# Masked scores written back to their PSUM bank in a banded attention chain, with a new instruction order

## The chip, the cores and the metric

One core of one Trainium2 chip runs the kernel. The metric is device time in microseconds (us) of one execution; the kernel was timed in three runs.

## What is computed

Attention with 16 heads-times-batches of 768 positions and 64 channels, followed by two dense layers pairs on the 1536 tokens of 512 channels that come out of it.

```python
scores = scale * np.matmul(q, k.transpose(0, 1, 3, 2))
keep = is_sink | in_window            # 4 sink columns, a causal window of 128
scores = np.where(keep, scores, -1e9)
scores = scores - np.max(scores, axis=-1, keepdims=True)
a = np.exp(scores)
a = a / (np.sum(a, axis=-1, keepdims=True) + 1e-09)
x = np.matmul(a, v)                   # -> (1536, 512)
h = x @ w_in                          # 512 -> 2048
g = np.where(h >= 1, h, np.where(h <= -1, 0, (h + 1) ** 2 / 4))
y = g @ w_out                         # 2048 -> 512
gate = 1 / (1 + np.exp(-(y @ w_gate)))
out = (gate * (y @ w_val)) @ w_out2   # 512 -> 1536 -> 512
```

## The kernel before

**Tiling.** The window is so narrow that 112 queries see 16 sink columns and at most 240 others, so a tile of 112 queries (the last of a batch has 96) has at most 256 columns of keys. Two batches of 7 tiles give tiles 0 to 13. Each tile is worked in four *slots* (`p`), and a slot is a pair of heads (`e` is 0 or 1). The first tile of a batch has 128 columns instead of 256.

**One slot.** TensorE (PE) multiplies queries and keys of both heads into two PSUM banks (`scores`, L927); two slots share these two banks, each taking one half (`j`) of both. VectorE (DVE) adds the mask, multiplies by -0.125 and takes the row minimum in one custom instruction (`top`, L930, by the helper at L1186), which writes the scaled scores to the SBUF tile `pr`. ScalarE (ACT) takes exponentials with that minimum as bias and sums the rows (`exp`, L933), in place in `pr`; a second short instruction reads out the sum. PE transposes the result into a PSUM tile (`turn`, L941), ScalarE copies that to SBUF (`pts`, by the helper at L358), and PE multiplies with the values (L968), for four slots in one piece. So a full tile has 8 tops, 8 exponentials, 4 copies of `pts`.

**End of a tile.** VectorE inverts the row sums `sm` (L982, L983), some engine widens them to `ie` (a copy), PE transposes `ie` (L991), ScalarE copies the output out of PSUM to `on`, VectorE multiplies the two (L1003), and `on` is split into `xh` and the remainder `xl` (L365), the two halves that the dense layers multiply with. A copy may be placed on ScalarE (L358), VectorE (L360) or GpSimd (POOL, L362).

**The dense layers.** The rest of the kernel is nearly all PE work: each product is three matmuls (high by high, high by low, low by high). The first stage for the first 512 tokens (`block`, L551 to L553 and L596 to L598, in pieces of 6 and 9 matmuls) is interleaved with the attention; its first piece needs `xl` of tile 4. Weights come as raw words (`st`, 512 KB each) on SyncE's DMA queue, behind queries, keys and values, and each is rebuilt on ScalarE or GpSimd (L452, L454), then in four VectorE instructions (L457 to L466), then split in two.

**Order.** Every step is an `op` with an engine (or several to choose from), an assumed duration, a due time, and keys that it reads and writes. A list scheduler (`Plan.order`) walks through assumed time: when an engine is free it starts the ready step with the earliest due time, and when a step can go on several engines it takes the one that ends first, with `BIAS` added. The order in which it starts steps is the order in which instructions are written out, and each engine executes its own in that order. `FINISH`, `MOE_DUE`, `MOE_PACE`, `EARLY`, `LATE`, `SAME_MODE` shift due times. Buffers are rings; PSUM's 8 banks are shared by scores, transposes, outputs and the dense layers, and a bank is given out again when its last user in the plan has ended. The real waits are set by the framework below, from the memory that each instruction touches; for PSUM it counts a whole bank as one.

Of the kernel before, what the change touches and what calls it, by code (L numbers as in the profile page):

```python
# [14 lines left out]
AF = mybir.ActivationFunctionType  # L15
# [3 lines left out]
P = 128  # L19
# [33 lines left out]
START = {"ACT": 0.9, "DVE": 2.1, "PE": 1.0, "SP": 1.1}  # L53
READY = {"tops": 0.2, "next": 0.5, "values": 1.5}

BIAS = {"DVE": 0.38, "POOL": 0.06, "ACT": -0.07}

SLOT_DUE = 2.55

FINISH = {"top": 3.59, "exp": 11.24, "turn": 13.87, "pts": 4.86, "values": -2.54, "div": 5.08, "out": -6.02}  # L60
MOE_DUE = 65.7
MOE_PACE = 5.86
DRAIN = 8.5
EARLY = 15.01
LATE = 62.91

ENTER, LEAVE = {"rows": 0.18, "cols": 0.14}, 0.09
SCORES_OF = 2
VALUES_OF = 4
SAME_MODE = 4.27  # L70
WARM = 6
RAW = 3
POOL_FROM = 5
# [11 lines left out]
def a_us(n):  # L85
    return 0.093 + n / 1200


def d1_us(n):
    return 0.068 + n / 1920  # L90


def d2_us(n):
    return 0.068 + n / 960


def g1_us(n):
    return 0.16 + n / 1195
# [14 lines left out]
def cells(name, row, c0, c1):  # L113

    return [(name, row, c) for c in range(c0 // 16, -(-c1 // 16))]
# [26 lines left out]
class Plan:  # L142
# [11 lines left out]
    def op(self, eng, dur, due, fn, reads=(), writes=(), lat=0.0, after=(), port=False, mode=None, uses=()):  # L154
        o = Op()
        o.on = eng if isinstance(eng, dict) else {eng: dur}
        o.pick = isinstance(eng, dict)

        o.port = port or "POOL" in o.on
        o.due, o.fn, o.lat, o.mode = due, fn, lat, mode  # L160
        o.n, o.deps, o.next, o.new = len(self.ops), set(after), [], []
        o.start = o.end = None
        for k in reads:
            if k in self.writer:
                o.deps.add(self.writer[k])
            self.readers.setdefault(k, []).append(o)
        for k in writes:
            if k in self.writer:
                o.deps.add(self.writer[k])
            elif isinstance(k, Buf) and not k.users:  # L170
                o.new.append(k)
            o.deps.update(self.readers.get(k, ()))
            self.writer[k], self.readers[k] = o, []
        o.deps.discard(o)

        o.new += [k for k in uses if not k.users]
        o.bufs = {k for k in (*reads, *writes, *uses) if isinstance(k, Buf)}
        for k in o.bufs:
            k.users.append(o)
        self.ops.append(o)  # L180
        return o

    def order(self):
# [16 lines left out]
        def room(o, t):  # L200
            if any(b.users[0] is not o and b.users[0].start is None for b in o.bufs):
                return False
            for b in o.new:
                r = b.ring
                if b.at - r.taken >= sum(c.ring is r for c in o.new):
                    return False
                if b.at >= r.n and not over(r.asked[b.at - r.n], t):
                    return False
            return all(len(idle(b.ring, t)) >= len(o.new) for b in o.new if b.ring.banks)
# [9 lines left out]
        def begin(o, e):  # L219

            t = max(free[e], now)
            return max(t, held["POOL" if e == "DVE" else "DVE"]) if o.port and e in held else t

        def best(o, e):

            return all(begin(o, x) + o.on[x] + BIAS.get(x, 0.0) >= begin(o, e) + o.on[e] + BIAS.get(e, 0.0) for x in o.on if x != e)

        while done < len(self.ops):
# [13 lines left out]
            for e in engines:  # L242
                if free[e] > now:
                    continue
                can = [(o.due - (SAME_MODE if e == "PE" and o.mode == mode else 0.0), o.n, o) for t, o in ready[e] if t <= now and best(o, e) and room(o, now)]
                if not can:
# [56 lines left out]
class Body:  # L303
# [205 lines left out]
    def W(self, nm, i, due):  # L509

        while self.asked <= self.first[nm, i]:
            self.load(*self.loads[self.asked], due - (EARLY if self.asked < 2 * STAGES[0] else LATE))
            self.asked += 1
# [326 lines left out]
    def banded(self):  # L840


        nc, NP, op, pre = self.nc, self.NP, self.plan.op, self.pre
# [16 lines left out]
        ot_r = self.bank_ring(OT_BANKS, P, NP, TQ)  # L860
        moe_due = [MOE_DUE, MOE_PACE]
        D = P // 2
        ot = sm = sc = None

        def slot(k, due):
            nonlocal ot, sm, sc
            t, p = slots[k]
            b, i, q0, n = tiles[t]
            ks = 1 if i == 0 else 2
            at = 1 if t < RAW else i % 2  # L870
            mask = masks.of(i, at)
# [26 lines left out]
            j = p % 2  # L898
# [4 lines left out]
            banks, o, sums = sc, ot, sm  # L903
            pt, pts = Buf(pt_r), Buf(pts_r)
            pr, mx = (Buf(pr_r), Buf(mx_r)) if t else (Kept(pre["rows"](p)), Kept(pre["mx"][:, 2 * p:2 * p + 2]))
            in_ring = [pr, mx] if t else []
            at_pr = [] if t else cells("acc", 0, pre["pr"][p], pre["pr"][p] + 2 * P)
# [19 lines left out]
                    nc.tensor.matmul(out=out, lhsT=own()[es, :n], rhs=rhs, start=True, stop=True)  # L927

            def top(e):
                row_tops(nc, pr.ap[:n, e, :ks * P], banks[e].ap[:n, j, :ks * P], mask[:n, :ks * P], mx.ap[:n, e:e + 1])  # L930

            def exp(e):
                nc.scalar.activation(  # L933
                    out=pr.ap[:n, e, :ks * P], in_=pr.ap[:n, e, :ks * P], func=AF.Exp,
                    bias=mx.ap[:n, e:e + 1], scale=-1.0, accum_out=sums.ap[:n, 2 * p + e:2 * p + e + 1],
                )

# [5 lines left out]
            f, m = ks / 2, ks * P  # L943
            if t:
                yield 0.43 * f, scores, rq, [(x, j) for x in sc], sc
            for e in range(2):
                if t == 0:
                    op("PRE", 0.0, 0.0, lambda: None, [], [(pr, e), (mx, e)], lat=READY["tops"] + 0.22 * (2 * p + e))
                    continue
                tops.append(op("DVE", d2_us(m) + 0.01, due - FINISH["top"], lambda e=e: top(e), [(banks[e], j), ("mask", min(i, 2))], [(pr, e), (mx, e)], uses=[banks[e], *in_ring]))  # L950
            for e in range(2):
                op("ACT", a_us(m) + 0.185, due - FINISH["exp"], lambda e=e: exp(e), [(mx, e)], [(pr, e), (sums, 2 * p + e), *at_pr], uses=[*in_ring, sums])
            op("PE", 0.38 * f + 0.02, due - FINISH["turn"], turn, [(pr, 0), (pr, 1), *at_pr], [pt], uses=in_ring[:1])

            def take(e):
# [5 lines left out]

            op({"ACT": a_us(4 * f * n), "DVE": d2_us(4 * f * n)}, 0, due - FINISH["pts"], take, [pt], [pts])

# [11 lines left out]
            if p == NP - 1:  # L975
# [21 lines left out]
                m = NP * n  # L997
                op("DVE", 0.28, due - FINISH["div"], inverse, [(sm, h) for h in range(H)], [sm], port=True)
                pool = t >= POOL_FROM
                op(self.some(pool, ACT=a_us(NP * P), DVE=d1_us(NP * P), POOL=g1_us(NP * P)), 0, due - FINISH["div"], widen, [sm], [ie], port=True)  # L1000
                op("PE", 0.38, due - FINISH["div"], spread, [ie], [ib])
# [12 lines left out]
        tops = []  # L1014
        for k in range(0, len(slots), NP):
            if k == NP:
                op("DVE", 1.25, SLOT_DUE * (NP - 2), masks.make_second, [], [("mask", 1)])
            if k == 2 * NP:
                op("DVE", 0.6, SLOT_DUE * (2 * NP - 2), masks.make_others, [("mask", 1)], [("mask", 2)])
            tile = [slot(k + j, SLOT_DUE * (k + j)) for j in range(NP)]  # L1020
            for j in range(0, NP if k else 0, SCORES_OF):
                both(tile[j:j + SCORES_OF], SLOT_DUE * (k + j), "rows")
                if VALUES_OF == 2:
                    both(tile[j:j + 2], SLOT_DUE * (k + j + 1) - FINISH["values"], "cols")
            if VALUES_OF == NP:
                both(tile, SLOT_DUE * (k + NP - 1) - FINISH["values"], "cols")
            for x in tile:
                next(x)
# [156 lines left out]
def row_tops(nc, out, x, mask, top):  # L1185
    nc.vector.tensor_tensor_reduce(out=out, in0=x, in1=mask, op0=ALU.add, op1=ALU.min, scale=-0.125, scalar=3.0e38, accum_out=top)  # L1186
# [138 lines left out]
```

## Time and profile before

| | before |
|---|---|
| median of 3 runs (lowest to highest) | 629.18 us (629.06 to 630.4) |
| the profiled execution's own time | 628.65 us |
| its span | 626.9 us |
| PE busy | 617.7 us (99%) |
| weight loads of PE busy | 540.1 us (86%) |
| VectorE busy | 509.4 us (81%) |
| ScalarE busy | 322.1 us (51%) |
| GpSimd busy | 90.3 us (14%) |
| granted TensorE clock in all 40 slices | 9 of 9 tenths |

Busy times count an instruction from start to acknowledged end, and neighbours overlap, so 99% does not say that PE has nothing to gain: the chain of waits, and the times at which instructions start, say where it stands still. Attention takes about the first 105 us; ScalarE is busy for 51% of the span on average but nearly all the time there.

### The profile page before, as it was taken

How to read it: one execution, taken by the hardware profiler on the slowest of the kernel's cores; microseconds unless marked ns; L12 is line 12 of the kernel's file. 1: busy time of each engine (PE TensorE's matmuls, PEld its weight loads, DVE VectorE, ACT ScalarE, POOL GpSimd, SP SyncE). 2: the span in 40 equal slices, each digit the busy share in tenths (PEclk: the TensorE clock that was granted, in tenths of full speed). 3: DMA queues.
4: the chain of work that ended last, by engine and by line, in shares of the span. 5: the costliest groups of instructions: out<-in, count | busy, mean ns of one | idle time of the engine just before them, and what ended most of it. 6: DMA issues, size and time to landing. Idle time of an engine off the chain costs nothing.

```text
span 626.9 us, 9877 instructions
## 1 busy us (share of the span) xinstructions
PE 617.7 (99%) x3532; PEld 540.1 (86%) x3532; DVE 509.4 (81%) x1103; ACT 322.1 (51%) x738; POOL 90.3 (14%) x114
## 2 busy tenths in 40 slices
PE   8999999999999999999999999999999999999996
PEld 6788888888888888888888999998998998998995
DVE  5899998999996984458968797698898898895373
ACT  6999997656532441234335576563452452541430
POOL 1103320301000330012014320011011111120000
PEclk9999999999999999999999999999999999999999
DMA  6876764151540310001300012221221222100004
GB/s 200 261 214 195 231 183 158 62 198 38 167 135 4 114 55 30 1 0 35 101 35 0 1 35 98 72 101 33 81 89 54 81 68 78 58 0 1 1 36 172
DMA packets 28571, 54.48 MB, mean 87 GB/s; under 512 B 3296, under 2 KB 18400, under 8 KB 28512
## 3 DMA queue, kind: packets, MB, share of 16 engines
q1 hardware_dynamic: 27648, 53.10, 26.0%
q8 instruction: 30, 0.49, 0.3%
q10 hardware_dynamic: 864, 0.66, 0.3%
q14 instruction: 29, 0.24, 0.1%
HBM read 50.60 MB, written 3.15 MB: 86 GB/s over the span
## 4 chain that ended last, share of the span: by engine, by line
PE 95%; DMA 2%; SPq 2%; DVE 0%; ACT 0%; issue 0%; POOL 0%; POOLq 0%
PE bank L713 28%; PE bank L596 7%; PE bank L551 7%; PE bank L552 7%; PE bank L597 7%; PE bank L598 7%; PE bank L553 7%; PE bank L800 5%; PE bank L801 5%; PE bank L799 5%; PE bank L968 3%; PE bank L941 3%; PE bank L927 2%; SPq L874 1%; DMA st<-in_w 1%; PE bank L991 1%
## 5 line engine op out<-in xcount | busy, mean ns | idle before, releaser
L713 PE MATMUL bank<-xh,early 128*128 128x384 f32 x384 | 107.3, 334 | 0.0
L713 PE MATMUL bank<-late,early 128*128 128x384 f32 x432 | 85.0, 335 | 0.0
L713 PEld LDWEIGHTS bank<-late,early 128*128 128x128 f32 x432 | 76.0, 188 | 0.9
L358 ACT ACTIVATE early<-w 128x512 fp32r<-128x512 f32 (+1 forms) x59 | 35.4, 601 | 78.4 <-PE bank L713 34.6
L713 PEld LDWEIGHTS bank<-xh,early 128*128 128x128 f32 x384 | 70.2, 188 | 0.2
L713 PE MATMUL bank<-xl,early 128*128 128x384 f32 x192 | 64.2, 334 | 0.0
L809 DVE TENSOR_TENSOR acc<-bank,acc 128x512 f32<-128x512 f32 (+1 forms) x61 | 40.6, 677 | 23.8 <-PE bank L801 23.7
L570 ACT ACTIVATE tmp<-tmp 128x512 f32<-128x512 f32 x48 | 30.2, 631 | 46.5 <-DVE tmp L567 46.3
L933 ACT ACTIVATE pr<-pr,mx 112x256 f32<-112x256 f32 (+2 forms) x104 | 50.9, 494 | 0.1
L452 ACT ACTIVATE w<-st 128x512 f32<-128x512 f32 x60 | 39.4, 668 | 21.7 <-DMA st<-in_w 8.2
L463 DVE SCALAR_TENSOR_TENSOR w<-st,w 128x512 int32<-128x512 int32 x68 | 48.1, 708 | 0.7
L466 DVE SCALAR_TENSOR_TENSOR w<-st,w 128x512 int32<-128x512 int32 x68 | 46.9, 690 | 0.7
L365 DVE TENSOR_TENSOR early<-w,early 128x512 fp32r<-128x512 f32 (+1 forms) x63 | 40.4, 643 | 4.4 <-ACT early L358 4.4
L567 DVE TENSOR_SCALAR tmp<-bank 128x512 f32<-128x512 f32 x48 | 32.6, 683 | 14.0 <-PE bank L553 13.7
L358 ACT ACTIVATE gs<-tmp 128x512 fp32r<-128x512 f32 (+1 forms) x51 | 31.7, 623 | 23.3 <-DVE tmp L573 22.4
L612 DVE TENSOR_TENSOR acc<-bank,acc 128x512 f32<-128x512 f32 x36 | 24.3, 688 | 22.3 <-PE bank L598 22.2
L365 DVE TENSOR_TENSOR gs<-tmp,gs 128x512 fp32r<-128x512 f32 (+1 forms) x51 | 36.7, 723 | 6.4 <-ACT gs L358 5.8
L551 PE MATMUL bank<-xh,early 128*128 128x512 f32 x96 | 38.1, 397 | 0.0
L1186 DVE CUSTOM_DVE_ANT_0 pr<-bank,mask 112x256 f32<-112x256 f32 (+2 forms) x104 | 37.6, 403 | 0.5 <-PE bank L927 0.3
L596 PE MATMUL bank<-gs,early 128*128 128x512 f32 x96 | 37.9, 395 | 0.0
L552 PE MATMUL bank<-xl,early 128*128 128x512 f32 x96 | 37.5, 390 | 0.0
L553 PE MATMUL bank<-xh,early 128*128 128x512 f32 x96 | 37.5, 390 | 0.0
(179 smaller groups left out, 1490.2 us busy)
## 6 DMA issues: line engine op xcount, KB each, us to landing
st<-in_w SPq DMA_DIRECT2D x32, 512.0 KB, 3.5
v<-in_vb SPq DMA_DIRECT2D x52, 128.0 KB, 3.0
qk<-in_qk SPq DMA_DIRECT2D x48, 128.0 KB, 3.2
st<-in_wg SPq DMA_DIRECT2D x12, 512.0 KB, 3.3
st<-in_wv SPq DMA_DIRECT2D x12, 512.0 KB, 3.2
st<-in_wo SPq DMA_DIRECT2D x12, 512.0 KB, 3.3
out<-acc SPq DMA_DIRECT2D x11, 256.0 KB, 2.2
acc<-in_qk SPq DMA_DIRECT2D x8, 128.0 KB, 3.3
```

The costliest lines, as they stand in the source:

```text
L358: self.nc.scalar.activation(out=out, in_=x, func=AF.Copy)
L365: (self.nc.vector if e == "DVE" else self.nc.gpsimd).tensor_tensor(out=out, in0=x, in1=y, op=ALU.subtract)
L463: nc.vector.scalar_tensor_tensor(out=t(), in0=high(), scalar=-0x80000000, in1=t(), op0=ALU.bitwise_and, op1=ALU.bitwise_or)
L466: nc.vector.scalar_tensor_tensor(out=t(), in0=low(), scalar=29, in1=t(), op0=ALU.logical_shift_right, op1=ALU.bitwise_or)
L551: mm(out=out, lhsT=wh[:, c], rhs=mh, start=k == 0, stop=False)
L552: mm(out=out, lhsT=wh[:, c], rhs=ml, start=False, stop=False)
L553: mm(out=out, lhsT=wl[:, c], rhs=mh, start=False, stop=k == KD - 1)
L596: mm(out=out, lhsT=wh[:, c], rhs=gh, start=f == fs[0], stop=False)
L597: mm(out=out, lhsT=wh[:, c], rhs=gl, start=False, stop=False)
L598: mm(out=out, lhsT=wl[:, c], rhs=gh, start=False, stop=f == fs[-1])
L713: nc.tensor.matmul(out=out, lhsT=w[:, c], rhs=m, start=start and i == n == 0, stop=i == 1 and n == 2, skip_group_check=True)
L933: nc.scalar.activation(out=pr.ap[:n, e, :ks * P], in_=pr.ap[:n, e, :ks * P], func=AF.Exp, bias=mx.ap[:n, e:e + 1], scale=-1.0, accum_out=s ...
```

## The change

`top` writes its scaled scores back over the scores in their PSUM bank, and `exp` reads them there and writes `pr` in SBUF. Tile 0, whose tops are made ahead of the plan, keeps them in SBUF. In the plan, a score bank is now used until the exponential has read it, and a `pr` buffer only from the exponential on; the assumed length of an exponential is 0.043 us shorter. Eleven numbers that set the order are new.

```diff
-BIAS = {"DVE": 0.38, "POOL": 0.06, "ACT": -0.07}
+BIAS = {"DVE": 0.337, "POOL": 0.09, "ACT": -0.08}
...
-FINISH = {"top": 3.59, "exp": 11.24, "turn": 13.87, "pts": 4.86, "values": -2.54, "div": 5.08, "out": -6.02}
-MOE_DUE = 65.7
-MOE_PACE = 5.86
+FINISH = {"top": 1.63, "exp": 8.595, "turn": 12.374, "pts": 5.372, "values": -2.493, "div": 3.461, "out": -6.051}
+MOE_DUE = 62.408
+MOE_PACE = 5.136
...
             def top(e):
-                row_tops(nc, pr.ap[:n, e, :ks * P], banks[e].ap[:n, j, :ks * P], mask[:n, :ks * P], mx.ap[:n, e:e + 1])
+                x = banks[e].ap[:n, j, :ks * P]
+                row_tops(nc, x, x, mask[:n, :ks * P], mx.ap[:n, e:e + 1])
 
             def exp(e):
                 nc.scalar.activation(
-                    out=pr.ap[:n, e, :ks * P], in_=pr.ap[:n, e, :ks * P], func=AF.Exp,
+                    out=pr.ap[:n, e, :ks * P], in_=banks[e].ap[:n, j, :ks * P] if t else pr.ap[:n, e, :P], func=AF.Exp,
                     bias=mx.ap[:n, e:e + 1], scale=-1.0, accum_out=sums.ap[:n, 2 * p + e:2 * p + e + 1],
                 )
...
-                tops.append(op("DVE", d2_us(m) + 0.01, due - FINISH["top"], lambda e=e: top(e), [(banks[e], j), ("mask", min(i, 2))], [(pr, e), (mx, e)], uses=[banks[e], *in_ring]))
+                tops.append(op("DVE", d2_us(m) + 0.01, due - FINISH["top"], lambda e=e: top(e), [("mask", min(i, 2))], [(banks[e], j), (mx, e)], uses=[banks[e], *in_ring[1:]]))
             for e in range(2):
-                op("ACT", a_us(m) + 0.185, due - FINISH["exp"], lambda e=e: exp(e), [(mx, e)], [(pr, e), (sums, 2 * p + e), *at_pr], uses=[*in_ring, sums])
+                scored = [(banks[e], j)] if t else []
+                op("ACT", a_us(m) + (0.142 if t else 0.185), due - FINISH["exp"], lambda e=e: exp(e), [(mx, e), *scored], [(pr, e), (sums, 2 * p + e), *at_pr], uses=[*in_ring, *([banks[e]] if t else []), sums])
```

The order moves on every engine. Three places matter below. The first is VectorE at the first weight chunk, after 20 tops (L1186 before, L1188 now) of tiles 1 to 3; `w` is the weight being rebuilt (L457, L460), `on`, `sm` and `xh` belong to a tile's end. Before:

```order
L1186 ISA pr,mx<-bank_93,mask_114 112x256
L1186 ISA mx 112x1
L457 TENSOR_SCALAR w<-w 128x512
L1003 TENSOR_TENSOR on<-on,bank_98 128x448
L982 TENSOR_SCALAR sm<-sm 112x8
L983 RECIPROCAL sm<-sm 112x8
L1186 ISA pr,mx<-bank_95,mask_114 112x256
```

Now:

```order
L1188 ISA bank_95,mx<-bank_95,mask_114 112x256
L1188 ISA mx 112x1
L1005 TENSOR_TENSOR on<-on,bank_96 128x448
L984 TENSOR_SCALAR sm<-sm 112x8
L985 RECIPROCAL sm<-sm 112x8
L457 TENSOR_SCALAR w<-w 128x512
L460 TENSOR_SCALAR w<-w 128x512
L360 CAST xh<-on 128x4x112
```

The weight's first step has moved behind the end of tile 1 and the inverse of tile 2, and its second step has moved up behind it, ahead of the next tops.

The second place is PE in the same stretch, at the end of tile 1 (L941 is `turn`, L942 now; L968 the values, L970 now; L991 the transposes of `ie`, L993 now). Before:

```order
L927 MATMUL bank_96<-qk_190 112x256
L927 MATMUL bank_93<-qk_190 112x256
L927 MATMUL bank_96<-qk_194 112x256
L927 MATMUL bank_93<-qk_194 112x256
L991 MATMUL bank_98<-ident,ie 128x112 x4
L941 MATMUL bank_94<-ident,pr 128x112 x4
L968 MATMUL bank_99<-pts,v 64x112 x16
L941 MATMUL bank_92<-ident,pr 128x112 x4
```

Now:

```order
L927 MATMUL bank_94<-qk_190 112x256
L927 MATMUL bank_95<-qk_190 112x256
L927 MATMUL bank_94<-qk_194 112x256
L927 MATMUL bank_95<-qk_194 112x256
L970 MATMUL bank_99<-pts,v 64x112 x16
L993 MATMUL bank_96<-ident,ie 128x112 x4
L942 MATMUL bank_92<-ident,pr 128x112 x4
L942 MATMUL bank_93<-ident,pr 128x112 x4
```

A tile's values no longer stand behind the transposes of the widened inverse but ahead of them; it is the same in tile 2.

The third place is VectorE in tile 2, where the first two tops have been made and the end of tile 0 stands between; the brackets name the engine whose semaphore is waited for. Before:

```order
L365 TENSOR_TENSOR xl<-on,xh 128x4x112
L1186 ISA pr,mx<-bank_98,mask_114 112x256
L1186 ISA mx 112x1
L360 COPY ie<-sm 112x512 [waits DVE_49]
L1186 ISA pr,mx<-bank_99,mask_114 112x256
L1186 ISA mx 112x1
```

Now:

```order
L365 TENSOR_TENSOR xl<-on,xh 128x4x112
L1188 ISA bank_92,mx<-bank_92,mask_114 112x256 [waits Activation_49]
L1188 ISA mx 112x1
L360 COPY ie<-sm 112x512 [waits DVE_49]
L1188 ISA bank_93,mx<-bank_93,mask_114 112x256 [waits Activation_49]
L1188 ISA mx 112x1
```

The rows stand in the same order, but the second slot's tops now wait for ScalarE, which reads the first slot's scores in the same bank. Of the 104 tops in the plan 22 wait for ScalarE now, 1 did before.

## Rows read from the trace of the kernel before

**Rows 1.** The three engines and the DMA by stretch: busy us, granted clock (view of windows).

```profile
core 0: us, PE busy (x) PEld busy (x) DVE busy (x) ACT busy (x) POOL busy (x), PEclk, DMA share, GB/s
...
16.00:32.00 16.00, 14.79 (x158) 11.33 (x157) 13.63 (x61) 14.78 (x52) 2.02 (x3) 1.00 0.81 258
...
48.00:64.00 16.00, 16.00 (x159) 13.02 (x154) 15.90 (x61) 15.72 (x57) 5.32 (x7) 1.00 0.70 211
```

**Rows 2.** Whole list of what PE waited for between 32 and 621 us (view of waits).

```profile
PE bank L991 <- ACT pr L933: 0.2, 1, 0.2
```

**Rows 3.** The chain that ended last: start us, us, what (view of the chain).

```profile
16.43 5.95 DMA st<-in_w
...
22.54 0.68 POOL w L454
...
23.25 0.43 DVE w L457
...
25.26 0.35 DVE ie L360
...
25.66 0.60 PE bank L991 x4
...
44.47 0.26 PE bank L551
...
44.76 0.51 PE bank L552
...
56.02 0.43 PE bank L551
...
56.45 0.23 PE bank L552
...
73.94 1.68 PE bank L968 x32
```

**Rows 4.** VectorE in order of time: start us, us, instruction, idle before (timeline).

```profile
23.25 0.43 DVE L457 TENSOR_SCALAR w<-w 128x512 f32<-128x512 f32 x1 [2.27 <-POOL w L454]
...
41.37 0.68 DVE L463 SCALAR_TENSOR_TENSOR w<-st,w 128x512 int32<-128x512 int32 x1
...
42.62 0.57 DVE L1003 TENSOR_TENSOR on<-on,bank 128x448 f32<-128x448 f32 x1
...
44.09 0.61 DVE L365 TENSOR_TENSOR xl<-on,xh 128x448 fp32r<-128x448 f32 x1
```

**Rows 5.** ScalarE in order of time, the same columns (timeline).

```profile
26.74 0.55 ACT L358 ACTIVATE pts<-bank 128x448 f32<-128x448 f32 x1 [0.38 <-PE bank L941]
...
29.00 0.54 ACT L358 ACTIVATE on<-bank 128x448 f32<-128x448 f32 x1 [0.73 <-PE bank L968]
...
41.28 0.55 ACT L358 ACTIVATE on<-bank 128x448 f32<-128x448 f32 x1
...
42.15 0.50 ACT L933 ACTIVATE pr<-pr,mx 96x256 f32<-96x256 f32 x1
...
65.96 0.50 ACT L933 ACTIVATE pr<-pr,mx 112x256 f32<-112x256 f32 x1
```

**Rows 6.** Costs by line and shape: count, busy us, mean ns (groups of instructions).

```profile
L933 ACT ACTIVATE pr<-pr,mx 112x256 f32<-112x256 f32 x80 | 39.8, 502 | 0.1
...
L358 ACT ACTIVATE ie<-sm 96x512 f32<-96x512 f32 x1 | 0.6, 617 | 0.0
...
L358 ACT ACTIVATE pts<-bank 128x224 f32<-128x224 f32 x7 | 2.2, 337 | 0.0
...
L754 ACT ACTIVATE rest<-rest 128x384 f32<-128x384 f32 x24 | 12.5, 525 | 12.1 <-DVE rest L745 11.8
...
L754 ACT ACTIVATE rest<-bank 128x384 f32<-128x384 f32 x18 | 8.4, 489 | 3.8 <-PE bank L713 3.4
...
L360 DVE COPY bank<-bank 128x384 f32<-128x384 f32 x2 | 1.1, 567 | 2.5 <-PE bank L713 2.5
...
L406 DVE TENSOR_TENSOR rest<-rest,bank 128x384 f32<-128x384 f32 x18 | 9.5, 546 | 2.9 <-PE bank L713 2.7
```

More of the change, by code (lines that the diff above doesn't have):

```diff
@@ L54 @@
 READY = {"tops": 0.2, "next": 0.5, "values": 1.5}
-BIAS = {"DVE": 0.38, "POOL": 0.06, "ACT": -0.07}
+BIAS = {"DVE": 0.337, "POOL": 0.09, "ACT": -0.08}
 SLOT_DUE = 2.55
-FINISH = {"top": 3.59, "exp": 11.24, "turn": 13.87, "pts": 4.86, "values": -2.54, "div": 5.08, "out": -6.02}
-MOE_DUE = 65.7
-MOE_PACE = 5.86
+FINISH = {"top": 1.63, "exp": 8.595, "turn": 12.374, "pts": 5.372, "values": -2.493, "div": 3.461, "out": -6.051}
+MOE_DUE = 62.408
+MOE_PACE = 5.136
 DRAIN = 8.5
-EARLY = 15.01
-LATE = 62.91
+EARLY = 19.969
+LATE = 63.205
 ENTER, LEAVE = {"rows": 0.18, "cols": 0.14}, 0.09
@@ L69 @@
 VALUES_OF = 4
-SAME_MODE = 4.27
+SAME_MODE = 4.18
 WARM = 6
```

## The prediction

> **What bounds the kernel now.** I read the stretches first. Between 48 and 64 us PE, VectorE and ScalarE are all busy for 98 to 100% of the time at the full granted clock; between 16 and 32 us none is, though ScalarE's 14.78 of 16 us is close to it [rows 1]. So the attention stage has three nearly full engines, and the next question is which of them waits. The view of waits answers it: from 32 us to 621 us PE waits once, for 0.2 us [rows 2]. After 32 us PE simply executes its list, and that list has the same matmuls before and after the change. The time can fall only by what PE loses ahead of the steady part, or by cheaper switching between kinds of matmul; it can rise by any new wait of PE.
>
> The chain that ended last shows what happens early. It goes from a weight DMA issued at 16.43 us (5.95 us long) over GpSimd's first rebuilding step to VectorE's first weight step at 23.25, and on to the widened inverse (25.26) and PE's transposes of it at 25.66 [rows 3]. VectorE had stood still for 2.27 us in front of that weight step [rows 4], while the end of tile 1, the inverse of tile 2 and further tops stood behind it in its queue. PE's list had the transposes of `ie` ahead of the values of tile 2, so PE stood still too; ScalarE then lost 0.38 and 0.73 us waiting for PE [rows 5]. Apart from these it had work one after another. The first piece of the dense layer marks the end of this part: PE starts it at 44.47 and its first matmul on `xl` of tile 4 at 44.76 [rows 3], right behind the VectorE instruction that makes this `xl`, which began at 44.09 [rows 4]. That in turn goes back to ScalarE's copy of tile 4's output at 41.28 [rows 5].
>
> **The change part by part.** I work out how much sooner that first matmul on `xl` can start, then what the rest adds.
>
> *The exponentials.* The same function with the same shape on ScalarE, the sigmoid of L754, takes 525 ns from SBUF and 489 ns from PSUM [rows 6]: 36 ns less. With 104 exponentials changed that is 3.7 us of ScalarE in all; 41 of them stand ahead of the copy of tile 4's output in the new order, so 41 x 0.036 = 1.48 us there. The bounds are 0 and 0.05 us each (a tenth of the 502 ns of one [rows 6]).
>
> *What ScalarE takes over.* Counted in the two orders ahead of that copy, ScalarE now has one more exponential, two more `pts` copies (one of 448, one of 224 columns) and one `ie` copy. By their durations less some 0.1 us that overlaps with the next instruction (a copy that starts at 41.28 lasts 0.55, yet two copies take until 42.15 [rows 5], 0.44 each) they cost 0.40 + 0.44 + 0.24 + 0.52 = 1.60 us [rows 6]. So ScalarE's own work up to there is 0.1 us more, not less: the saving is spent on copies that VectorE and GpSimd had. Over the whole attention stage GpSimd goes from 120 to 99 instructions.
>
> *The stall.* What can come back is the 1.11 us that ScalarE waited for PE, since its cause is moved: the end of tile 1 and the inverse now stand ahead of the weight step, and PE's values ahead of the transposes of `ie`. VectorE will still wait for the same DMA, whose place in SyncE's queue is unchanged, but behind it stand then tops of tile 3, which ScalarE needs only some 2 us later. I take 1.0 of 1.11 (0 to 1.11).
>
> *From the copy to `xl`.* Before, 3.48 us lie between 41.28 and 44.76. About 0.8 of it is VectorE finishing two weight steps from 41.37 before it multiplies at 42.62 [rows 4], though the copy had ended at 41.83. Now one weight step stands there, and the next one, a top and `xh` (on ScalarE) share the way to `xl`. I take 0.4 us sooner (0 to 0.8).
>
> *VectorE's write to PSUM.* No top wrote to PSUM before. The nearest rows are a copy from bank to bank, 567 ns, and an instruction with a bank as one input and SBUF as output, 546 ns, both with 384 columns [rows 6]. So a top costs 0 to 0.021 us more, 0 to 2.2 us for 104; below nothing is excluded by the order of these rows. I take nothing, since the difference lies within the end that overlaps the next instruction; if it were on the path, some 45 tops ahead of the first piece would cost up to 0.9 us. Here a page of the Trainium skill speaks against the change: "Perfetto Trace Analysis", Optimizing Scalar/DVE Operations, puts VectorE's fixed cost at about 60 ns on SBUF and 125 ns on PSUM. Were the output's place to count as that says, 104 x 65 ns = 6.8 us (an estimate from that page) would fall on VectorE, against 2.2 us by the row; no run here shows it yet.
>
> *Bank by bank.* Ahead of the first piece 7 tops now wait until ScalarE has read the other slot of their bank, and exponentials wait for both slots' tops. Each such wait is between nothing and one exponential (0.50 us [rows 6]): 0 to 3.5 us. I take 0.2, because ScalarE is mostly the later of the two.
>
> *After the first piece.* PE's list there changes between kinds of matmul 29 times instead of 25. The first dense matmul behind scores takes 0.43 us where the next takes 0.23 [rows 3], so a change costs up to 0.2 us, and four up to 0.8. I take 0.2, since most of the new ones only part one change in two. Moving pieces of the dense layer earlier costs nothing: PE is full there anyway. The cover for everything on VectorE and ScalarE is PE's lag: the last exponential of tile 9 starts at 65.96 [rows 5], its values at 73.94 [rows 3], 8 us later. By the instructions counted in the two orders and their durations, ScalarE has, net of the saving, some 3 to 5 us more to do ahead of the exponentials of tiles 10 to 12 than before (weights, `ie`, `xh`), which eats into that; if the cover is gone, each further us is a us of the end. The score banks are held until the exponentials now; PE's next scores would be late first, and PE's waits would show it.
>
> *Sum.* 0.1 (work) - 1.0 (stall) - 0.4 (way to `xl`) + 0.2 (banks) + 0.2 (changes) = -0.9, and I round up to 1.0 for the ScalarE ends that lean the same way. The profiled execution took 628.65 us, 1.75 more than its span, 0.53 below the median. 628.65 - 1.0 = 627.65; on the median's footing 628.2.
>
> **The rivals.** The bound for telling a difference is 0.2%, 1.26 us.
>
> *All of it passes.* The stall goes (1.11), the way to `xl` is 0.8 shorter, the exponentials save 0.05 each (0.6 more), the banks cost nothing: 0.1 - 1.11 - 0.8 - 0.6 = -2.4, 626.8. For it speaks that PE itself could reach the first piece about 1 us sooner or more, since early values gain from the new order; against it, that ScalarE hands its gain to copies.
>
> *The change doesn't do what it says.* ScalarE, full as it is, reaches the copy of tile 4 at the same time, because the copies it takes over outweigh the 36 ns: 629.2. For it speaks the sum of +0.1 us above.
>
> *Slower: VectorE and ScalarE take turns at a bank.* 22 tops wait for an exponential. It decides when the waits ahead of the first piece exceed the 1.4 us won there, or the later ones exceed PE's lag. With half of the bound, 7 x 0.25 = 1.75 early, and 15 x 0.25 = 3.75 later on top of 3 to 5 us of displaced work against a lag of 8 us, of which about half is needed for the transposes, copies and pieces in between and 4 is free; say 2 us of it reaches the end: 629.2 - 1.2 + 1.75 + 2 = 631.7; with a third of it 630.5. I put 630.8. For it speaks that both engines are full and had been decoupled by six `pr` buffers; against it, that ScalarE mostly trails VectorE. The Trainium skill states the rule behind it ("PSUM — Partial Sum Buffer", PSUM bank collisions raise a hardware error): two engines must not touch the same bank and quadrant at once, reads included, so a semaphore has to guard the bank, not the address. The waits written out in the new order agree.
>
> *Slower: the tops themselves.* If a top that writes to PSUM occupied VectorE longer, the 45 early ones would delay `xl` of tile 4 by 45 times the difference. With the bound of 0.021 us that is 0.9 us, which takes the gain back: 629.1. Twice the gain would be lost with 0.05 us each, 2.3 us: 630.5. For it speaks only that the two rows differ at all; against it, that a top reads PSUM already and its end overlaps the next.
>
> **How the numbers follow.** Forecast with its own range 627.2 to 629.0: 0.50, of which 0.20 lies below 627.92 (faster) and 0.30 above. All of it passes: 0.16, faster. No effect: 0.10, same. Turns at a bank: 0.20, slower. Longer tops: 0.04, of which 0.02 is slower. Together faster 0.36, same 0.42, slower 0.22. The range 626.2 to 630.8 takes in the lower rival and reaches to the slower one's value; it leaves out about 2 in 10.
>
> **What would show it.** Right: exponentials at about 0.466 us; ScalarE without the two waits near 26 and 29 us; VectorE's stall before its first weight step shorter than 2.27 us and with the end of tile 1 ahead of it; PE's first dense matmul on `xl` near 43.7 us; no wait of PE from there on; tops as long as now. Wrong: tops that are 0.02 us or more longer, VectorE idle in front of second tops with ScalarE as releaser, or PE waiting for exponentials or for scores' banks between 45 and 105 us. Then the time is above 629.

## The result, and the profile after

| | before | changed |
|---|---|---|
| median of 5 runs (lowest to highest) | 629.06 us (628.03 to 630.4) | 632.95 us (632.38 to 633.46) |
| ratio of the times, 95% interval | | 1.0067 (1.0055 to 1.0078) |
| the profiled execution, its span | 628.65, 626.9 us | 632.95, 631.1 us |
| VectorE busy | 509.4 us | 512.0 us |
| ScalarE busy | 322.1 us | 324.3 us |
| GpSimd busy | 90.3 us | 73.6 us |

The change makes the kernel 0.67% slower, about 4 us, where 1 us faster was forecast. Three views of the profile after, in the order of the prediction's steps. First the windows (columns as in [rows 1]); this line of the kernel before, for a stretch that [rows 1] leaves out, is for comparison:

```profile
64.00:80.00 16.00, 16.00 (x164) 13.48 (x163) 15.93 (x61) 15.86 (x51) 5.43 (x7) 1.00 0.76 229
```

The changed kernel:

```profile
16.00:32.00 16.00, 15.47 (x162) 12.13 (x160) 15.29 (x63) 15.04 (x55) 2.01 (x3) 1.00 0.78 245
48.00:64.00 16.00, 15.69 (x159) 12.40 (x154) 15.40 (x53) 14.86 (x53) 1.59 (x2) 1.00 0.70 211
64.00:80.00 16.00, 15.94 (x149) 12.83 (x149) 15.47 (x53) 14.58 (x48) 2.68 (x4) 1.00 0.60 186
```

The early stretch is fuller than in [rows 1], as forecast. But in the two stretches from 48 to 80 us VectorE, ScalarE and PE are all a little emptier, at the full granted clock: they lose time to something. The costs by shape, 5 to 110 us, first of the kernel before (its tops stand in no row above), then of the changed one (busy us, mean ns of one, idle before):

```profile
L1186 DVE CUSTOM_DVE_ANT_0 pr<-bank,mask 112x256 f32<-112x256 f32 x80 | 29.8, 414 | 0.5 <-PE bank L927 0.3
L1186 DVE DVE_READ_ACCUMULATOR2_ANT mx<- 112x1 f32 x96 | 7.7, 80 | 0.0
```

```profile
L934 ACT ACTIVATE pr<-bank,mx 112x256 f32<-112x256 f32 x80 | 38.8, 516 | 3.9 <-DVE mx L1188 3.7
L1188 DVE CUSTOM_DVE_ANT_0 bank<-bank,mask 112x256 f32<-112x256 f32 x80 | 32.1, 447 | 1.7 <-ACT pr L934 1.4
L1188 DVE DVE_READ_ACCUMULATOR2_ANT mx<- 112x1 f32 x96 | 13.0, 135 | 0.0
```

Both kinds of loss that were named as signs of a wrong prediction are there: tops are longer, and ScalarE and VectorE wait for each other. The view of waits has, over all shapes from 5 to 110 us (us in total, times, longest):

```profile
ACT pr L934 <- DVE mx L1188: 4.5, 9, 0.9
DVE bank L1188 <- ACT pr L934: 1.9, 6, 0.4
```

The exponentials' own mean (516 ns) is no shorter than in [rows 6]; their gain shows only from start to start, 0.45 us where it was 0.49, since the end of one overlaps the next. One turn, in VectorE's and then ScalarE's order of time:

```profile
59.28 0.43 DVE L1188 CUSTOM_DVE_ANT_0 bank<-bank,mask 112x256 f32<-112x256 f32 x1 [0.32 <-ACT pr L934]
59.63 0.47 DVE L1188 CUSTOM_DVE_ANT_0 bank<-bank,mask 112x256 f32<-112x256 f32 x1
```

```profile
58.70 0.46 ACT L934 ACTIVATE pr<-bank,mx 112x256 f32<-112x256 f32 x1
59.15 0.34 ACT L358 ACTIVATE pts<-bank 128x224 f32<-128x224 f32 x1
60.18 0.47 ACT L934 ACTIVATE pr<-bank,mx 112x256 f32<-112x256 f32 x1 [0.69 <-DVE mx L1188]
```

VectorE stands still until ScalarE has read the bank at 58.70 to 59.2; then ScalarE stands still until VectorE has made the tops that it is late with. From 55.9 to 79.5 us the chain that ended last now lies with VectorE and ScalarE, and goes through such pairs; in the kernel before it was PE's alone from 32 us on ([rows 3] shows places of it):

```profile
59.28 0.43 DVE bank L1188
...
69.36 0.32 DVE bank L1188
...
69.84 1.48 ACT pr L934 x6
...
77.91 0.56 ACT pr L934 x2
78.47 0.55 ACT tmp L570
79.02 0.44 ACT pts L358
79.50 2.46 PE bank L927 x16
```

### The profile page after: what moved, and what is told of

Its sections match the earlier page's. It is cut to its first block, busy times and chain, and to the rows that moved or that the text cites. A ratio compares the mean times of both kernels' runs of the same rounds, so it can differ in the third digit from the quotient of the medians.

```text
span 631.1 us, 9807 instructions
## 1 busy us (share of the span) xinstructions
PE 622.3 (99%) x3532; PEld 542.7 (86%) x3532; DVE 512.0 (81%) x1111; ACT 324.3 (51%) x751; POOL 73.6 (12%) x93
## 4 chain that ended last, share of the span: by engine, by line
PE 88%; DVE 5%; ACT 5%; DMA 1%; issue 0%; SPq 0%; ACTq 0%
PE bank L713 28%; PE bank L596 7%; PE bank L598 7%; PE bank L597 7%; PE bank L551 6%; PE bank L553 6%; PE bank L552 6%; PE bank L800 5%; PE bank L801 5%; PE bank L799 5%; ACT pr L934 3%; DVE bank L1188 2%; PE bank L927 2%; ACT pts L358 1%; PE bank L942 1%; PE bank L970 1%
## 5 line engine op out<-in xcount | busy, mean ns | idle before, releaser
L358 ACT ACTIVATE early<-w 128x512 fp32r<-128x512 f32 (+1 forms) x62 | 36.8, 596 | 77.9 <-PE bank L713 28.7
L934 ACT ACTIVATE pr<-bank,mx 112x256 f32<-112x256 f32 (+2 forms) x104 | 49.2, 499 | 4.6 <-DVE mx L1188 4.5
L452 ACT ACTIVATE w<-st 128x512 f32<-128x512 f32 x62 | 40.9, 670 | 19.0 <-DVE early L365 8.9
L463 DVE SCALAR_TENSOR_TENSOR w<-st,w 128x512 int32<-128x512 int32 x68 | 46.8, 692 | 0.5
L466 DVE SCALAR_TENSOR_TENSOR w<-st,w 128x512 int32<-128x512 int32 x68 | 46.6, 689 | 0.7
L365 DVE TENSOR_TENSOR early<-w,early 128x512 fp32r<-128x512 f32 (+1 forms) x63 | 44.2, 706 | 0.0
L1188 DVE CUSTOM_DVE_ANT_0 bank<-bank,mask 112x256 f32<-112x256 f32 (+2 forms) x104 | 40.6, 436 | 2.2 <-ACT pr L934 1.9
L596 PE MATMUL bank<-gs,early 128*128 128x512 f32 x96 | 37.9, 395 | 0.0
L598 PE MATMUL bank<-gs,early 128*128 128x512 f32 x96 | 37.4, 390 | 0.0
## 6 DMA issues: line engine op xcount, KB each, us to landing
st<-in_w SPq DMA_DIRECT2D x32, 512.0 KB, 3.3
st<-in_wg SPq DMA_DIRECT2D x12, 512.0 KB, 3.2
st<-in_wv SPq DMA_DIRECT2D x12, 512.0 KB, 3.2
st<-in_wo SPq DMA_DIRECT2D x12, 512.0 KB, 3.3
```

The costliest lines, as they stand in the source:

```text
L358: self.nc.scalar.activation(out=out, in_=x, func=AF.Copy)
L365: (self.nc.vector if e == "DVE" else self.nc.gpsimd).tensor_tensor(out=out, in0=x, in1=y, op=ALU.subtract)
L463: nc.vector.scalar_tensor_tensor(out=t(), in0=high(), scalar=-0x80000000, in1=t(), op0=ALU.bitwise_and, op1=ALU.bitwise_or)
L466: nc.vector.scalar_tensor_tensor(out=t(), in0=low(), scalar=29, in1=t(), op0=ALU.logical_shift_right, op1=ALU.bitwise_or)
L596: mm(out=out, lhsT=wh[:, c], rhs=gh, start=f == fs[0], stop=False)
L598: mm(out=out, lhsT=wl[:, c], rhs=gh, start=False, stop=f == fs[-1])
```

## The experiments

Three theories of the 4 us: the **price** of tops that write to PSUM, **turns** that VectorE and ScalarE take at a shared bank (not the step `turn`), and the **order** that the new numbers set. All ratios are to the kernel before, run beside each; its median was 628.96 to 629.32 us there. Exponentials that read the mask leave the scores out, those of no_price leave the mask out.

| kernel | order | tops write | exponentials read | median us | ratio (95% interval) |
|---|---|---|---|---|---|
| changed | new | bank | bank | 632.95 | 1.0067 (1.0055 to 1.0078) |
| order_alone | new | `pr` | `pr` | 629.53 | 1.0004 (0.9996 to 1.0013) |
| no_turns | new | bank | mask in SBUF | 630.85 | 1.0023 (1.0014 to 1.0031) |
| no_price | new | `pr` | bank | 631.56 | 1.0037 (1.0024 to 1.0051) |
| one_reader | new | bank | one slot mask, one bank | 630.53 | 1.0025 (1.0014 to 1.0035) |
| mixed | new | head 0 bank, head 1 `pr` | the same place | 630.63 | 1.0028 (1.0017 to 1.0040) |
| price_old_order | old | bank | mask in SBUF | 630.85 | 1.0026 (1.0017 to 1.0036) |
| one_head_in_bank | old | head 0 bank, head 1 `pr` | head 0 mask, head 1 `pr` | 629.21 | 1.0003 (0.9994 to 1.0012) |
| stall_alone | old, one row moved | `pr` | `pr` | 628.74 | 0.9999 (0.9990 to 1.0008) |
| numbers_alone | own plan, new numbers | `pr` | `pr` | 631.55 | 1.0037 (1.0023 to 1.0050) |
| path_old_numbers | own plan, old numbers | bank | bank | 637.95 | 1.0137 (1.0122 to 1.0152) |
| both_tops_first | own plan, other keys | bank | bank | 633.06 | 1.0068 (1.0055 to 1.0081) |
| before_again | old | `pr` | `pr` | 629.52 (one run) | |

**order_alone.** The changed plan, but the `pr` buffer is taken at the top:

```diff
 x = banks[e].ap[:n, j, :ks * P]
-row_tops(nc, x, x, mask...)
+if pr.ap is None:
+    pr.ap = pr.ring.make(pr.at % pr.ring.n)
+row_tops(nc, pr.ap[:n, e, :ks * P], x, mask...)
...
-in_=banks[e].ap[:n, j, :ks * P] if t else pr.ap[:n, e, :P]
+in_=pr.ap[:n, e, :ks * P]
```

> The changed kernel's instruction order, row for row on every engine, but with the old data path: tops write the scores to the pr tile in SBUF, exponentials read them there. Three theories of the 4 us that the change cost (632.95 against 629.06 us). Price: each of 104 tops holds VectorE some 37 ns longer when its output is a bank (3.9 us), so this kernel is back at about 629, or below by up to 1.4 for the stall that the order removes (627.6 to 629.2), tops about 0.345 us apart. Turns: the 19 tops more that wait for ScalarE, and the exponentials that wait for VectorE because PSUM is guarded by the bank, are the loss, and it is gone here too: 627.6 to 629.2. Order: the new numbers place work badly, whatever the data path; then it stays at about 633, or above it, since exponentials lose their 39 ns again.

629.53 us, ratio 1.0004: in this order the loss comes with the data path, and the order by itself gains nothing either. Its first matmul on `xl` starts at 45.19 us (44.76 in the execution that the prediction read).

**no_turns.** `in_=mask[:n, :ks * P] if t else ...`, with scale 1.0.

> The changed kernel's order row for row, tops write to the bank, but exponentials read the mask tile in SBUF in place of the bank (the scores are left out of the exponentials). The long tops stay, the waits of tops for exponentials fall from 22 to 3, and exponentials are back at SBUF's pace. Price: about 632 to 633.5, tops 0.38 us apart. Turns: about 629, ScalarE's 4.5 us and VectorE's 1.9 us of waiting for one another mostly gone. Order: about 633.

630.85 us, between the theories: 1.3 us above order_alone, 2.1 below the changed kernel.

**no_price.** Tops as in order_alone, exponentials on the bare scores in the bank, scale 0.125.

> The changed kernel's order row for row and its 22 waits of tops for exponentials, but tops write to the pr tile in SBUF, and exponentials read the bank that holds the bare scores (the mask is left out of the exponentials). The exponentials keep their 39 ns, only the tops' output is moved. Price: tops 0.345 us apart, 628 to 629.5. Turns: 632 to 633.5, since every wait at a bank is still there. Order: about 633.

631.56 us, 2.0 above order_alone, 1.4 below the changed kernel. So neither theory is whole: price and turns add up, 1.3 + 2.0 of 3.4 us.

The four kernels have one order, so their times compare place by place. The start of PE's values, in us (first matmul on `pts` of a tile, PE in order of time):

| | tile 2 | tile 4 | tile 8 | tile 10 | tile 13 |
|---|---|---|---|---|---|
| order_alone | 25.01 | 39.07 | 68.05 | 81.57 | 106.32 |
| no_turns | 25.16 | 39.21 | 68.41 | 82.60 | 107.36 |
| no_price | 25.81 | 40.36 | 69.51 | 83.41 | 108.23 |
| changed | 26.18 | 40.73 | 70.08 | 84.60 | 109.74 |

The price (no_turns over order_alone) is 0.1 us by tile 4 and 0.4 by tile 8; it appears by tile 10, with 1.0. Turns (no_price over order_alone) cost 0.8 us by tile 2 and 1.3 by tile 4, but part of that is made up: the first dense matmul starts 0.4 us later (45.21 against 44.85), the values of tile 6 0.3. Most of what stays is lost behind that, 1.5 by tile 8 and 1.9 by tile 13. The last column's 3.4 us is the difference of the spans (627.7 to 631.1), so nothing is lost or won back behind attention.

**one_reader.** `in_=mask... if t and not j else banks[e]...`

> The changed kernel's order row for row, tops write to the bank; only the second slot of each bank pair has its exponentials read the bank, the first slot's read the mask tile in SBUF (those exponentials leave the scores out). No second top then waits for an exponential of the first slot (3 waits of tops for ScalarE are left, as without any reader), and no first exponential for the second slot's tops, but PE still gets a bank for new scores only after the last two exponentials. Half of the exponentials keep the 39 ns. Turns between the two slots of a bank are the rest of the loss (what lies above the 630.85 us of the kernel without turns): then 630 to 631. Banks that come free late for PE are the rest: then 632 to 633.

630.53 us, as no_turns. Half of the exponentials save their 0.04 us (start to start 0.45 against 0.49) and by the plan PE's banks come free as late as in the changed kernel, and neither shows in the time. So the turns between two slots of a bank are what lies above the price.

**mixed.** The change for one head: `pr.ap[...] if e else x` as the tops' output, `banks[e]... if t and not e else pr...` as the exponentials' input.

> The changed kernel's order row for row, with the change made for the first head of each slot alone: its tops write to the bank and its exponentials read there; the second head's tops write to the pr tile and its exponentials work in place there, as before the change. Tops alternate between the two places, so the longer pitch should be gone (0.34 to 0.345 us); 13 tops wait for ScalarE, between the 3 and the 22 of the other two. If the turns cost in proportion: 2.0 us x 10/19 = 1.05 above the order alone, 630.3 to 630.9. If the waits that are left are all that matter, as much as in no_price: 631.5. A version that beats the old kernel needs less than 628, and nothing speaks for that.

630.63 us: half of the turns cost half, and tops start 0.344 us apart (mean of 48), so the price is gone. Of the forms here that compute the whole result it is the best, and still slower than before.

**price_old_order.** Only the tops' output is moved to the bank, in the old kernel.

> The old kernel's order row for row; the only edit that costs anything is that tops write to the bank, while exponentials read the mask tile in SBUF (scores left out). Tops 0.37 to 0.38 us apart against 0.34. If the longer tops reach the end in the old order as they do in the new one: 1.0 to 1.5 us more than before, 630.3 to 630.8. If the lag of PE covers them there, as the prediction took it: 629.3, within 0.5.

630.85 us, by the ratio 1.6 above before (1.1 to 2.3): the longer tops reach the end in the old order too. So the 4 us of free cover that the prediction took is not there.

**before_again.** The kernel before in a second execution.

> The old kernel, unchanged, profiled in a second execution. The question is whether the 2.27 us for which VectorE stood in front of its first weight step, and the 0.38 and 0.73 us of ScalarE behind it, belong to the kernel or to the one execution that the prediction read. If to the kernel: VectorE idle for 2 us or more there again, ScalarE's two waits too. If to the execution (in the kernel with the old order and longer tops the same step waited for 0.33 us, after a start of attention 0.7 us later): under 1.5 us, with ScalarE's waits shorter or gone, at the same time of 628 to 630.

629.52 us. The first weight step waits for nothing now (the same line in [rows 4] had 2.27 us in front of it), and ScalarE loses nothing around 26 to 29 us:

```profile
21.91 0.42 DVE L457 TENSOR_SCALAR w<-w 128x512 f32<-128x512 f32 x1
```

VectorE's first top came at 7.10 us here against 6.49 in the execution that the prediction read (the last section says why), and GpSimd began on the weight at 21.01 against 22.54. More important, VectorE has 8% of the chain that ended last in this execution, some 50 us, a full queue up to 79.18 us (by engine on the page, then the chain in order of time):

```profile
PE 90%; DVE 8%; DMA 1%; ACT 0%; issue 0%; SPq 0%
```

```profile
77.35 0.53 DVE on L1003
77.88 0.34 DVE pr L1186
...
78.22 0.34 DVE pr L1186
...
78.56 0.61 DVE tmp L573
...
79.22 0.60 PE bank L941 x4
```

`tmp` (L573) reads a dense block's bank, and PE's next transposes write to that bank. In VectorE's and PE's order of time, the execution that the prediction read has it like this:

```profile
77.98 0.68 DVE L573 TENSOR_TENSOR tmp<-tmp,bank 128x512 f32<-128x512 f32 x1
...
78.71 0.60 PE L941 MATMUL bank<-ident,pr 112*128 112x112 f32 x4
```

L573 ends at 78.66, PE starts at 78.71. The view of waits shows nothing there ([rows 2]), yet no margin is left: PE starts 0.05 us behind the end of L573 also in the two kernels below, where it is listed as waiting for it. In before_again the wait is long enough to be listed, and with longer tops it moves on with them:

```profile
79.22 0.60 PE L941 MATMUL bank<-ident,pr 112*128 112x112 f32 x4 [0.62 <-DVE tmp L573]
```

```profile
80.26 0.68 DVE L573 TENSOR_TENSOR tmp<-tmp,bank 128x512 f32<-128x512 f32 x1
...
81.00 0.60 PE L941 MATMUL bank<-ident,pr 112*128 112x112 f32 x4 [0.66 <-DVE tmp L573]
```

(The last two are price_old_order: L573 started at 78.49 in before_again, 80.26 here, 1.8 us later; the time rose by 1.6.)

**stall_alone.** The planned list of the kernel before with one row moved:

```diff
 order, end = self.order()
+if fill:
+    first = next(i for i, o in enumerate(order) if o.eng == "DVE" and o.fn.__name__ == "clamp")
+    to = next(i for i, o in enumerate(order) if i > first and o.eng == "DVE" and o.fn.__name__ == "widen")
+    order.insert(to, order.pop(first))
```

> The old kernel with one row moved: VectorE's first weight step stands behind the end of tile 1, the inverse and the widened inverse of tile 2 instead of ahead of them, so its 2.27 us of waiting for the weight has other work in front. Everything else is the old kernel, row for row. If the prediction's term for the stall is right (-1.0 us, and PE does nothing but its list from 32 us on): values of tile 2 start 1 to 2 us sooner and the time is about 1 us shorter, 628.0. If another engine makes up for it before the first piece of the dense layer, as the order by itself (629.53 against 629.32 us) suggests: values of tile 2 sooner, the first dense matmul at the same time, 629.0 within 0.4.

628.74 us, ratio 0.9999 (0.9990 to 1.0008): the row's place is worth nothing in the median. The values of tile 2 start at 27.22 us, no sooner than in before_again (27.08), so that expected sign is missing. GpSimd began on the weight at 20.82 in this execution, when VectorE was still at its tops: there was no stall to win back, and what moving the row is worth where there is one, the trace doesn't show.

**one_head_in_bank.** In the old kernel `row_tops(nc, pr.ap[...] if e else banks[e].ap[...], ...)`.

> The old order row for row; the tops of each slot's first head write to the bank, those of the second to the pr tile in SBUF, so that tops in a row alternate between the two places; exponentials of the first head read the mask tile in SBUF (they leave the scores out). Where all tops write to the bank, a top right behind another top takes 0.38 us to the next start and one behind anything else 0.34, as in SBUF. If every top that writes to a bank pays behind another top, whatever that one wrote: those of the first head take 0.38 behind tops, the others 0.345, and the time is about half of the way to price_old_order, 629.8. If it takes two bank-writing tops in a row: all at 0.34 to 0.35, and the time is that of before, 629.0 to 629.3.

629.21 us, ratio 1.0003, tops 0.34 to 0.35 us apart wherever they stand: the price needs two bank-writing tops in a row. VectorE's order of time in no_turns (0.38 us apart) and here (0.34 or 0.35):

```profile
20.83 0.47 DVE L1188 CUSTOM_DVE_ANT_0 bank<-bank,mask 112x256 f32<-112x256 f32 x1
21.21 0.14 DVE L1188 DVE_READ_ACCUMULATOR2_ANT mx<- 112x1 f32 x1
21.21 0.47 DVE L1188 CUSTOM_DVE_ANT_0 bank<-bank,mask 112x256 f32<-112x256 f32 x1
```

```profile
20.45 0.43 DVE L1186 CUSTOM_DVE_ANT_0 bank<-bank,mask 112x256 f32<-112x256 f32 x1
20.80 0.14 DVE L1186 DVE_READ_ACCUMULATOR2_ANT mx<- 112x1 f32 x1
20.80 0.42 DVE L1186 CUSTOM_DVE_ANT_0 pr<-bank,mask 112x256 f32<-112x256 f32 x1
21.14 0.08 DVE L1186 DVE_READ_ACCUMULATOR2_ANT mx<- 112x1 f32 x1
```

**The plans.** numbers_alone is the old code with the new numbers, path_old_numbers the new code with the old ones, and both_tops_first gives an exponential the keys of both slots:

```diff
+            yield None
             for e in range(2):
-                scored = [(banks[e], j)] if t else []
+                scored = [(banks[e], 0), (banks[e], 1)] if t else []
...
+            for x in tile:
+                next(x)
```

> The old data path with its own plan and the eleven new numbers alone (an order close to the changed kernel's, not the same). Price and turns: within 1.3 us of 629, perhaps 1 below for the early stall. Order: slower, towards 633.

> The new data path with the old eleven numbers. 16 tops wait for ScalarE in its order. Price and turns are the cause: slower than 629.3 by 2 us or more, 631.3 to 634. The new numbers are the cause (they made the old data path 2.2 us slower): near 629.5.

> The changed kernel with a plan that knows of the shared banks: an exponential needs the tops of both slots, so tops never stand behind exponentials of the same bank (1 wait of a top for ScalarE is left); the order is a new one. If turns at a bank are what costs beside the longer tops, and the new order is no worse: 630 to 631.5. If the scores' way from top to exponential is what counts, so that exponentials that start later cost as much as the turns did: 632.5 to 634.

631.55, 637.95 and 633.06 us. Numbers and data path go together: with the old ones the new path is 5 us slower still, beyond what was expected of either cause, and with the new ones the old path loses 2.2. Why, these two runs don't separate. Planning both tops ahead of the exponentials ends the waits of tops, but its first dense matmul starts at 48.48 us instead of 45.59, and the time stays the same; since that order differs everywhere, it does not say how much the turns were.

## Why the prediction was wrong

- **What bounds the kernel** is where it failed first. "After 32 us PE simply executes its list" does not hold: even in the execution that was read PE starts at 78.71 us when VectorE's L573 lets it, and in another the chain of the same kernel is VectorE's until 79 us. Two full engines at 98 to 100% [rows 1] were the sign of it; that PE had no wait in the list [rows 2] was no measure of what was free.
- **The gain ahead of the first piece** (-1.0 for the stall, -0.4 for the way to `xl`) did not come. The first matmul on `xl` was to start near 43.7 us; it starts at 45.92 in the changed kernel and at 45.19 in order_alone, which has neither price nor turns, against 44.76 and 44.30 in the two executions before. And although it is later in order_alone, the time is that of before, so this start does not set the end as the prediction had it.
- **The stall** went with the execution that was read. At the same step VectorE stood still for nothing in before_again, 0.3 us in price_old_order and 0.8 in one_head_in_bank. In order_alone the values of tile 2 do start 2.1 us sooner than in before_again (25.01 against 27.08), but the first dense matmul starts 0.9 us later (44.85 against 43.96), and the gain is gone by tile 4. In part it was never a gain: ahead of tile 2's values PE has made 40 transposes of `turn` and 8 of `ie` there, against 48 and 12; ahead of tile 4's it is 80 and 20 in both. That ScalarE's added copies take the rest, as the prediction's rival had it, fits (ScalarE is busy for 24.00 of the 24 us from 24 to 48 us there), but no run separates it.
- **VectorE's write to PSUM** was taken as nothing, with 0.021 us each as the most. It costs 0.037 us (0.382 against 0.345) where a top follows a top, 67 of 104 in the new order, and nothing elsewhere: 67 x 0.037 = 2.5 us on VectorE, 1.3 us at the end in the new order (no_turns over order_alone), 1.6 in the old. The nearest rows could not show it: the only two copies from bank to bank stand alone, 8 us apart. The rival of longer tops had the cost and, with its 0.05 us each (630.5), about its size, at 4% of the chance; but it looked for the delay ahead of `xl` of tile 4, and by tile 4 it is 0.1 us. The estimate from the Trainium skill ("Perfetto Trace Analysis", Optimizing Scalar/DVE Operations), 65 ns for each top and 6.8 us in all, does not fit either: tops that stand alone pay nothing, nor do those that alternate between bank and SBUF.
- **Bank by bank** was taken as 0.2 us ahead of the first piece, and as nothing behind it. Ahead of it that was near: 0.4 us by the first dense matmul (no_price over order_alone). Behind it the turns go on, to 2.0 us at the end. The mean was put low because "ScalarE is mostly the later of the two". It is, but only by having a queue of tops ready, and a top that waits for ScalarE uses up that queue, as in the turn at 59.28: ScalarE's waits for tops (4.5 us) are more than VectorE's for ScalarE (1.9 us), and order_alone has neither. The rule of the Trainium skill ("PSUM — Partial Sum Buffer", PSUM bank collisions raise a hardware error), that a bank has to be guarded as a whole, agrees with these waits. The rival of turns was right about the mechanism. The two rivals were priced one at a time; both came, and together they pass the 630.8.
- **The exponentials**: the size was right, 0.04 us each by start to start, against 36 ns. Its worth did not show: with half of them saving it (one_reader) the time is that of none (no_turns), within the noise.
- **After the first piece**: the cover of 4 us was read from exponentials to values, 8 us apart [rows 3, 5]. The shortest way from VectorE to PE is another, over a bank that the dense layer's `tmp` frees, and it has no cover at 78.71 us. So longer tops reach the end in the old order (price_old_order, 1.6 us).

So four terms failed: the gain of 1.4 us ahead of the first piece, which the new order by itself does not give; the longer tops, put at nothing; the turns, put at 0.2; and the cover that was to hide what comes later. The sum as measured: order 0.2, price 1.3, turns net of the saving 2.0, together 3.5 of the 3.9 us between the medians; the 0.4 that is left lies within the intervals, each some 0.1% (0.6 us) to either side.

Not tried: a layout in which a bank holds both heads of one slot, so that no two slots share one.

## What to carry to other kernels

Before a wait in one profile is priced, look whether a second execution of the same kernel has it; and where two engines are full, look for the smallest margin between them and the next engine at shared buffers, not for listed waits. Here an output moved from SBUF to PSUM cost nothing alone and something in a row, and alternating destinations took that away. Two engines that work on one bank lose their buffers between them: count the waits that the order writes out as stalls for the engine behind as well.

## What was unexpected of the hardware

In the same order, a 112x256 top that follows another takes 0.345 us to the next start with its output in SBUF (36 of them) and 0.382 with it in a bank (36); behind any other instruction 0.340 and 0.342 (16 each); alternating between bank and SBUF 0.344 to 0.345 (mixed). The short instruction that reads out the row minimum is listed with 0.14 us behind a bank-writing top and 0.08 us behind one that writes to SBUF, also where tops alternate and nothing is paid, so its listed length is no sign of the cost.

Executions of one kernel start attention 0.6 us apart, and TensorE's clock is what differs. PE's 16 matmuls for the first scores, in the execution that the prediction read and in before_again, make the whole 0.6 us:

```profile
5.02 1.44 PE L1242 MATMUL bank<-acc 64*112 64x128 f32 x16 [0.73 <-DMA acc<-in_qk]
```

```profile
5.02 2.05 PE L1242 MATMUL bank<-acc 64*112 64x128 f32 x16 [0.74 <-DMA acc<-in_qk]
```

The view of windows prints a granted clock of 1.00 here in both. But the trace's own record of that clock begins only at 4.21 us in the first and at 10.61 us in the second, and ahead of it the printed 1.00 rests on no record. The matmuls show the level: pairs of the next scores (L927) start 216 ns apart in the first, from 6.9 us on, and 427 ns apart in the second up to 9.9 us, half the rate, so there the clock was at the lower of its two levels (1.2 and not 2.4 GHz). In the changed kernel the pairs go from 427 to 216 ns at 8.9 us, where its record begins (8.88). Of the 14 profiled executions three have the higher level before 5 us and the first scores in 1.42 to 1.44 us; the other eleven have it from 8.5 us or later, and 2.05. The execution that the prediction read was one of the three, and in another of them (numbers_alone) VectorE stood still in front of its first weight step for 2.02 us, much as for the 2.27 of [rows 4]. In both kinds PE had made 12 matmuls from 1.35 us on and then waited 0.7 us for data; what decides when the clock rises, no run shows.
